# Attention's product with v: f32 exponentials as the moving operand instead of f16 pairs as weights

## The chip, the cores and the metric

The kernel runs on one core of a Trainium2 chip. The metric is the device time of one execution in microseconds; three executions of the kernel before took 1527.67 to 1531.33 us, median 1530.16. The engines are named as in the profile: PE is TensorE (matmuls; PEld its weight loads), DVE is VectorE, ACT is ScalarE, POOL is GpSimd, SP is SyncE, which issues DMAs. TensorE works on weights, which lie in the array, and on a moving operand that streams past them a column at a time; results go to PSUM, which has 8 banks.

## The reference

Attention with cluster masks, then two MoE layers; all inputs are f32.

```python
# attention: batch 2, 8 heads, 768 positions, head_dim 64, 16 centroids per head
q_assign = np.argmax(np.einsum('bhsd,hcd->bhsc', q_n, c_n), axis=-1)   # q_n, k_n, c_n: normalized
k_assign = np.argmax(np.einsum('bhsd,hcd->bhsc', k_n, c_n), axis=-1)
mask = q_assign[:, :, :, None] == k_assign[:, :, None, :]
scores = scale * np.matmul(q, k.transpose(0, 1, 3, 2))
scores = np.where(mask, scores, -1000000000.0)
scores = scores - np.max(scores, axis=-1, keepdims=True)
attn = np.exp(scores)
attn = attn / (np.sum(attn, axis=-1, keepdims=True) + 1e-09)
x = np.matmul(attn, v)                                  # rearranged to 1536 x 512
# first MoE: h = x @ w_in; x = (h * clip(h + 3, 0, 6) / 6) @ w_out
# second MoE: 8 experts relu(x @ w1[e]) @ w2[e], weighted by a balanced softmax of x @ w_gate
```

## The kernel before, in words

f32 precision is kept with pairs of f16 numbers: a value is split into its f16 rounding and the f16 of the rest, and a product of two values takes three f16 matmuls (hi x hi, hi x lo, lo x hi).

Attention runs over 16 heads (`i`), two to a pair (`p`), and over 6 tiles of 128 keys each (`c`); one tile of one head is a unit, numbered `g`, 96 in all. The loop at L952 writes out the instructions of all engines in a fixed order, unit by unit; each engine then works through its own list in that order. In iteration `g` stand:

- `max_unit` for the unit 8 ahead (L659): two matmuls of 384 columns write the masked scores that are needed for the row maximum to the tile `pmt`, two banks of PSUM which exist once, and VectorE reduces them (L675). The next unit's matmuls overwrite `pmt`.
- `e_split` for the unit before (L732): the exponentials E, f32, are cast to f16 (Eh, on ScalarE, every fourth or so on VectorE, L738), and GpSimd subtracts (El, L742).
- `s_mm` (L711): four matmuls of 384 columns make the scores of 128 keys and 768 queries, and ScalarE takes the exponential of all 768 (L729).
- `pv_mm` for the unit 4 behind (L745, the distance is `LAG`): the product with v. Weights are blocks of 128 queries of Eh and El, moving is v: 65 columns (v's high part and a column of ones, which sums the exponentials) and 64 (its low part). The result `pv` lies with queries on partitions. In a head's last unit the term `Wt` is added, which makes good for rows whose cluster has no key.
- `weave` (L695): preparation steps of later pairs at the units that the table `PLACE` names (f16 splits of q and k, cluster choice, v's pair in `vhi` and `vlo`, the sums `abs1` and `abs2` behind `Wt`), the decoding of the first MoE weight (`w00`), and a head's evacuation (`evac_tasks`, L774): division by the sum, f16 split, and transposing DMAs into `xT` (L800).

A step that waits on an engine holds up all that stands behind it on that engine. Behind the loop the first MoE layer's matmuls follow (`l1_mm`, L898; 36 of them don't need the last pair's `xT`).

Of the kernel before, what the change touches and what calls it, by code (L numbers as in the profile page):

```python
# [31 lines left out]
def attention_moe_kernel(  # L32
# [39 lines left out]
    one = const.tile([P, 1], F32, name="one")  # L72

# [327 lines left out]
    ps_s = actx.enter_context(tc.tile_pool(name="ps_s", bufs=2, space=PSUM))  # L401
    ps_v = actx.enter_context(tc.tile_pool(name="ps_v", bufs=2, space=PSUM))
# [3 lines left out]
    NU = NHEAD * NJ  # L406
    qnA = [ap1.tile([P, 2 * NJ, P], F16, name=f"qnA{i}") for i in range(NA)]
    knA = [ap1.tile([P, 2 * NJ, P], F16, name=f"knA{i}") for i in range(2)]
    Wt = [ap1.tile([P, 2, 130], F16, name=f"Wt{i}") for i in range(2)]
# [62 lines left out]
    def prep_tasks(p, parts=None):  # L472
# [47 lines left out]
        def vhi():  # L520
            vn = d["vn"] = ap3.tile([P, 2 * NJ, 130], F16, tag="vn", name=f"vn{p}")
            nc.scalar.activation(vn[:, :, 0:D], vr, AF.Copy, scale=sv[0][:, 0:1])
            nc.gpsimd.memset(vn[:, :, D:D + 1], 1.0)

        def vlo():
            vn = d["vn"]
            nc.vector.scalar_tensor_tensor(
                out=vn[:, :, D + 1:2 * D + 1], in0=vr, scalar=sv[0][:, 0:1], in1=vn[:, :, 0:D],
                op0=ALU.mult, op1=ALU.subtract)
# [129 lines left out]
    def max_unit(i, j):  # L659
# [7 lines left out]
        ps = ps_s.tile([P, 2, 512], F32, tag="s", name=f"pm{i}_{j}") if early else pmt  # L667
# [41 lines left out]
    pvt = {}  # L709

    def s_mm(i, c):  # L711

        p, hh = divmod(i, 2)
        d = st[p]
        ps = ps_s.tile([P, 2, 512], F32, tag="s", name=f"pS{i}_{c}")
# [4 lines left out]
        for g in range(2):  # L720
            nc.tensor.matmul(
                ps[:, g, 0:N2], lhsT=d["kB"][:, t, :], rhs=qb[:, hh * S + g * N2:hh * S + (g + 1) * N2],
                start=True, stop=False)
        for g in range(2):
            nc.tensor.matmul(  # L725
                ps[:, g, 0:N2], lhsT=d["kA"][0:KR, t, :], rhs=qa[0:KR, g * N2:(g + 1) * N2],
                start=False, stop=True)
        E = ap2.tile([P, 2, N2], F32, tag="E", name=f"E{i}_{c}", bufs=3)
        nc.scalar.activation(E, ps[:, :, 0:N2], AF.Exp, scale=d["esc"][:, 0:1])  # L729
        EE[i, c] = E  # L730

    def e_split(i, c):  # L732
        E = EE.pop((i, c))
        Eh = ap3.tile([P, 2, N2], F16, tag="Eh", name=f"Eh{i}_{c}", bufs=5)
        El = ap3.tile([P, 2, N2], F16, tag="El", name=f"El{i}_{c}", bufs=5)
        n = NJ * i + c
        if n % 12 in (0, 3, 5) or n >= NU - LEAD and n % 2:
            nc.vector.tensor_copy(Eh, E)  # L738
        else:
            nc.scalar.copy(Eh, E)  # L740
        for g in range(2):
            nc.gpsimd.tensor_tensor(out=El[:, g], in0=E[:, g], in1=Eh[:, g], op=ALU.subtract)  # L742
        EE[i, c] = (Eh, El)

    def pv_mm(i, c):  # L745
        p, hh = divmod(i, 2)
        d = st[p]
        if c == 0:
            pvt[i] = ps_v.tile([P, NJ, D + 1], F32, tag="v", name=f"pv{i}")
        ps = pvt[i]  # L750
        Eh, El = (x.rearrange("p a b -> p (a b)") for x in EE.pop((i, c)))
        vn = d["vn"][:, hh * NJ + c, :]

        def acc(j, w, r, lo=False, **kw):
            r = r[:, D + 1:2 * D + 1] if lo else r[:, 0:D + 1]
            kw = {"start": False, "stop": False, **kw}
            nc.tensor.matmul(ps[:, j, 0:r.shape[1]], lhsT=w, rhs=r, skip_group_check=True, **kw)

        for j in range(NJ):
            w = Eh[:, P * j:P * j + P]  # L760
            acc(j, w, vn, start=(c == 0 and j == 0))
            acc(j, w, vn, lo=True)
        for j in range(NJ):
            acc(j, El[:, P * j:P * j + P], vn)
        if c == NJ - 1:
            for j in range(NJ):
                w = d[f"qA2_{hh}"][0:D + C, j, :]
                r = Wt[p % 2][0:D + C, hh]
                acc(j, w, r)
                acc(j, w, r, lo=True, stop=(j == NJ - 1))  # L770
# [42 lines left out]
    nc.gpsimd.memset(one, 1.0)  # L813
    c0()
# [103 lines left out]
    LAG = 4  # L918
    tasks, evacs = {}, {}
# [23 lines left out]
    for c in range(FA):  # L943
# [6 lines left out]
        if c + 2 < FA:  # L950
            at(u + 3, wcols[c + 2][1][0])
    for g in range(-LEAD, NU + LAG + 16):  # L952
        i, u = divmod(g, NJ)
        chains = []
        if 0 <= g + LEAD < NU:
            chains.append(max_unit(*divmod(g + LEAD, NJ)))
        if 0 <= g - 1 < NU:
            e_split(*divmod(g - 1, NJ))
        if 0 <= g < NU:
            s_mm(i, u)  # L960
# [7 lines left out]
        if 0 <= gp < NU:  # L968
            pv_mm(*divmod(gp, NJ))
        if 0 <= gp < NU and gp % NJ == NJ - 1:  # L970
            for n, f in enumerate(evac_tasks(gp // NJ)):
                evacs.setdefault(g + (1, 2, 2)[n], []).append(f)
# [670 lines left out]
```

## Time and profile before

| | |
|---|---|
| Median of three runs | 1530.16 us |
| Span of the profiled execution | 1526.7 us |
| Lowest and highest run | 1527.67 and 1531.33 us |
| PE, DVE, ACT, POOL busy over the span | 93%, 63%, 44%, 25% |
| POOL El L742 | 192 instructions, 189.3 us |
| Granted clock in the slices of 38 us up to 305 us | 0.7 to 0.9, from then on nearly always 0.9 or more |

The profiled execution's own time is its span and some 1 us around it (the fastest run is 0.97 us above the span). The shares are averages over a short part in which no engine is full (attention, the first fifth of the span) and a long one in which PE is. A view by windows gives for each stretch the busy time of PE, PEld, DVE, ACT and POOL, the number of instructions in brackets, then the mean granted clock (1 is 2.4 GHz), the DMA's share and GB/s. A timeline row has its start and its length in us, engine, line, operation, out<-in, the shape, how many it stands for, and in brackets the idle time before it. A group's row ends with busy us and mean ns of one, and behind the bar with idle time before it and what ended that. A PE record's length goes on past the point at which the next matmul starts, so the distance of two starts is what a matmul costs.

### The profile page before, as it was taken

The page shows a single profiled execution, that of the slowest core. Times are in us where ns is not written, and L with a number is a line of the kernel's source. Part 1 is how long each engine was busy: PE and PEld are TensorE (multiplying, and loading weights), DVE is VectorE, ACT ScalarE, POOL GpSimd, SP SyncE. Part 2 cuts the span into 40 slices and gives each one's busy share as a digit, 9 for nine tenths or more (in the row PEclk, how much of TensorE's full clock was granted, in tenths as well). Part 3 has the DMA queues.
Part 4 walks back from the last instruction along what each step waited for, and adds up shares of the span by engine and source line. Part 5 has one row for each costly group of instructions (what it writes and reads, how often), then busy time and mean ns, then how long its engine had stood idle before and what let it go on. Part 6 is the DMA issues. An engine that isn't in the chain of part 4 may idle for free.

```text
span 1526.7 us, 22967 instructions
## 1 busy us (share of the span) xinstructions
PE 1418.7 (93%) x9289; PEld 764.8 (50%) x9289; DVE 955.4 (63%) x1732; ACT 665.3 (44%) x1123; POOL 387.8 (25%) x427
## 2 busy tenths in 40 slices
PE   3878888898999998999999999999999999999998
PEld 1555556543444444544555555555555555555554
DVE  7889898876756866466565466466456565564333
ACT  2677777475553444343344333333333333324221
POOL 1579889752101321030030020020020020021000
PEclk9799899898999998999999999999999999999999
DMA  9675743331321100101101101101101101100011
GB/s 217 145 162 102 134 87 62 91 116 52 129 69 56 56 0 1 55 1 56 56 1 55 56 1 56 56 1 56 55 1 55 56 1 55 38 19 1 1 42 42
DMA packets 106633, 87.60 MB, mean 57 GB/s; under 512 B 78368, under 2 KB 88608, under 8 KB 106528
## 3 DMA queue, kind: packets, MB, share of 16 engines
q1 hardware_dynamic: 106528, 86.15, 20.8%
q8 instruction: 72, 1.18, 0.3%
q14 instruction: 33, 0.27, 0.1%
HBM read 64.01 MB, written 3.15 MB: 44 GB/s over the span
## 4 chain that ended last, share of the span: by engine, by line
PE 71%; DVE 17%; ACT 5%; issue 4%; DMA 1%; POOL 0%; DVEq 0%; ACTq 0%; POOLq 0%; SPq 0%
PE o L1471 11%; PE o L1472 11%; PE o L1470 11%; PE X L1521 5%; PE X L1524 5%; PE X L1523 5%; PE Y L1521 4%; PE Y L1524 4%; PE Y L1523 4%; DVE pmt L675 3%; PE l L1248 2%; PE pmt L672 1%; PE l L912 1%; PE l L913 1%; PE l L914 1%
## 5 line engine op out<-in xcount | busy, mean ns | idle before, releaser
L1472 PE MATMUL o<-w_s,hl 128*128 128x512 f16 x768 | 291.6, 380 | 0.0
L1471 PE MATMUL o<-w_s,hh 128*128 128x512 f16 x768 | 291.5, 380 | 0.0
L1470 PE MATMUL o<-w_s,hh 128*128 128x512 f16 x768 | 291.3, 379 | 0.0
L1540 ACT ACTIVATE hh<-u 128x384 f16<-128x384 f32 x192 | 100.3, 522 | 374.9 <-DVE u L1536 374.9
L742 POOL TENSOR_TENSOR El<-E,Eh 128x384 f16<-128x384 f32 x192 | 189.3, 1014 | 72.8 <-DVE Eh L738 41.2
L1541 DVE SCALAR_TENSOR_TENSOR hl<-u,hh 128x384 f16<-128x384 f32 x192 | 112.8, 587 | 120.1 <-ACT hh L1540 120.1
L1536 DVE TENSOR_TENSOR u<-X,snap 128x384 f32<-128x384 f32 x64 | 35.7, 557 | 189.5 <-PE X L1524 189.5
L121 POOL PARTITION_ALL_REDUCE w_m<-w_mx x14 | 5.4, 383 | 570.2 <-DVE w_mx L1336 332.7
L1523 PEld LDWEIGHTS <-wop 128*128 128x128 f16 x896 | 87.9, 98 | 93.6 <-issue 13.5
L1521 PEld LDWEIGHTS <-wop 128*128 128x128 f16 x896 | 87.9, 98 | 81.9 <-issue 1.1
L1536 DVE TENSOR_TENSOR u<-Y,snap 128x384 f32<-128x384 f32 x128 | 70.8, 553 | 80.1 <-PE Y L1524 79.1
L1472 PEld LDWEIGHTS <-hl 128*128 128x128 f16 x768 | 75.2, 98 | 90.8 <-issue 0.3
L1248 PE MATMUL l<-hh,w_s 128*128 128x512 f16 x384 | 118.3, 379 | 0.0
L1524 PEld LDWEIGHTS <-wop 128*128 128x128 f16 x896 | 87.9, 98 | 58.5 <-issue 0.9
L729 ACT ACTIVATE E<-pS,esc 128x768 f32<-128x768 f32 x96 | 86.2, 900 | 65.7 <-PE pS L725 48.4
L1470 PEld LDWEIGHTS <-hh 128*128 128x128 f16 x768 | 76.0, 99 | 66.5 <-issue 0.2
L1529 ACT COPY snap<-X 128x384 f32<-128x384 f32 x128 | 61.2, 478 | 109.7 <-PE X L1524 108.3
L1471 PEld LDWEIGHTS <-hh 128*128 128x128 f16 x768 | 75.2, 98 | 66.5 <-issue 0.2
L675 DVE TENSOR_REDUCE pmt<-pmt 128x1 f32<-128x768 f32 x84 | 80.6, 960 | 19.5 <-PE pmt L672 18.7
L672 PE MATMUL pmt<-kA,qA 80*128 80x384 f16 x184 | 52.1, 369 | 42.5 <-DVE pmt L675 14.2
L1248 PEld LDWEIGHTS <-w_s 128*128 128x128 f16 x576 | 56.4, 98 | 67.5
L1521 PE MATMUL X<-xop,wop 128*128 128x384 f16 x256 | 83.8, 327 | 6.8 <-ACT snap L1529 5.5
(280 smaller groups left out, 2990.5 us busy)
## 6 DMA issues: line engine op xcount, KB each, us to landing
w_raw<-in_moe_w_dram SPq DMA_DIRECT2D x16, 2048.0 KB, 8.2
w_c<-in_moe_w_out_dram SPq DMA_DIRECT2D x16, 512.0 KB, 3.5
w00x<-in_moe_w_in_dram SPq DMA_DIRECT2D x8, 512.0 KB, 5.6
w00f<-in_moe_w_in_dram SPq DMA_DIRECT2D x8, 512.0 KB, 4.1
w_c<-in_moe_w_in_dram SPq DMA_DIRECT2D x8, 512.0 KB, 3.8
qraw<-in_q_dram SPq DMA_DIRECT2D x8, 384.0 KB, 3.8
kraw<-in_k_dram SPq DMA_DIRECT2D x8, 384.0 KB, 4.8
vraw<-in_v_dram SPq DMA_DIRECT2D x2, 1536.0 KB, 10.6
```

The source lines that it names most:

```text
L675: nc.vector.tensor_reduce(nmx[i][:, j:j + 1], ps[:, :, 0:N2], axis=AX.XY, op=ALU.max, negate=True)
L742: nc.gpsimd.tensor_tensor(out=El[:, g], in0=E[:, g], in1=Eh[:, g], op=ALU.subtract)
L1248: nc.tensor.matmul(po[i], lhsT=a, rhs=r, start=(f == 0 and z == 0), stop=(f == NFC - 1 and z == 2))
L1470: nc.tensor.matmul(pe2[t], lhsT=a, rhs=wh, start=first, stop=False)
L1471: nc.tensor.matmul(pe2[t], lhsT=a, rhs=wl, start=False, stop=False)
L1472: nc.tensor.matmul(pe2[t], lhsT=b, rhs=wh, start=False, stop=last)
L1521: nc.tensor.matmul(o[:, 0:XT], lhsT=wh, rhs=xh, start=(first and c == 0), stop=False, skip_group_check=True)
L1523: nc.tensor.matmul(o[:, 0:XT], lhsT=wh, rhs=xl, start=False, stop=False, skip_group_check=True)
L1524: nc.tensor.matmul(o[:, 0:XT], lhsT=wl, rhs=xh, start=False, stop=(c == 1), skip_group_check=True)
L1536: nc.vector.tensor_tensor(h, src, r[k], op=ALU.add)
L1540: nc.scalar.activation(hh, src, AF.Relu)
L1541: nc.vector.scalar_tensor_tensor(out=hl, in0=src, scalar=0.0, in1=hh, op0=ALU.max, op1=ALU.subtract)
```

## The change

The f16 pairs of the exponentials and of v are gone. The work is cut in halves `h` of 384 queries, 192 in all; within a head first the six key tiles of the first half, then those of the second. The scores of a half are two matmuls, its exponential is one of 384 columns. In the product with v the weights are v itself in f32 with two columns of ones (66 columns, `DW`), and the moving operand is E in f32, 384 columns. The result `pvT` has the 64 numbers and the sum on partitions and queries along the columns; `turn_tasks` copies it to SBUF on ScalarE and turns it back with three f32 transposes on PE per half, one and two units after the half's end, and the evacuation starts two units later than before (`TURN`). `Wt` is the weight of two f16 matmuls of 384 columns per half. The sums behind `Wt` are taken from v's sum over all keys, which GpSimd makes (`vsum`). PSUM is dealt anew: three one-bank tiles for scores, three for products. The tuple `SPLIT`, which would leave heads with the old pairs, is empty.

```diff
-    ps_s = actx.enter_context(tc.tile_pool(name="ps_s", bufs=2, space=PSUM))
-    ps_v = actx.enter_context(tc.tile_pool(name="ps_v", bufs=2, space=PSUM))
+    ps_v = actx.enter_context(tc.tile_pool(name="ps_v", bufs=3, space=PSUM))
...
+    DW = D + 2
+    SPLIT = ()
...
+            vn = d["vn"] = ap3.tile([P, 2 * NJ, DW], F32, tag="vn", name=f"vn{p}")
             nc.scalar.activation(vn[:, :, 0:D], vr, AF.Copy, scale=sv[0][:, 0:1])
...
-        def vlo():
+        def vsum():
+            vn = d["vn"].rearrange("p (h j) d -> p h j d", h=2)[:, :, :, 0:D]
+            t = ap2.tile([P, 2, 3, D], F32, tag="vs", name=f"vs{p}", bufs=1)
+            nc.gpsimd.tensor_tensor(out=t, in0=vn[:, :, 0:3], in1=vn[:, :, 3:6], op=ALU.add)
+            nc.gpsimd.tensor_tensor(out=t[:, :, 0], in0=t[:, :, 0], in1=t[:, :, 1], op=ALU.add)
+            nc.gpsimd.tensor_tensor(out=t[:, :, 0], in0=t[:, :, 0], in1=t[:, :, 2], op=ALU.add)
...
+            nc.tensor.matmul(
+                ps[:, :, 0:D], lhsT=one.to_broadcast([P, P]), rhs=t[:, :, 0], start=True, stop=True,
+                skip_group_check=True)
...
+    def s_mm(h):
+        i, x = divmod(h, 2 * NJ)
+        g, c = divmod(x, NJ)
...
+        nc.tensor.matmul(
+            ps, lhsT=d["kB"][:, t, :], rhs=qb[:, hh * S + g * N2:hh * S + (g + 1) * N2], start=True, stop=False)
+        nc.tensor.matmul(
+            ps, lhsT=d["kA"][0:KR, t, :], rhs=qa[0:KR, g * N2:(g + 1) * N2], start=False, stop=True)
+        E = ap2.tile([P, N2], F32, tag="E", name=f"E{h}", bufs=11)
+        nc.scalar.activation(E, ps, AF.Exp, scale=d["esc"][:, 0:1])
...
+        ps = pvT[i, g][0:DW]
+        nc.tensor.matmul(ps, lhsT=d["vn"][:, hh * NJ + c, :], rhs=E, start=(c == 0), stop=False)
         if c == NJ - 1:
+            q = qa.rearrange("p a b -> p (a b)")[0:D + C, g * N2:(g + 1) * N2]
+            nc.tensor.matmul(ps, lhsT=W[:, 0:DW], rhs=q, start=False, stop=False)
+            nc.tensor.matmul(ps, lhsT=W[:, DW:2 * DW], rhs=q, start=False, stop=True)
+
+    def turn_tasks(i, g):
+        x = {}
+        def t0():
+            o = x["o"] = ap2.tile([P, N2], F32, tag="oT", name=f"oT{i}_{g}")
+            nc.scalar.copy(o[0:DW], pvT.pop((i, g))[0:DW])
+        def t1():
+            if g == 0:
+                pvt[i] = ps_v.tile([P, NJ, DW], F32, tag="v", name=f"pv{i}")
+            for n in range(NJ // 2):
+                nc.tensor.matmul(
+                    pvt[i][:, 3 * g + n, :], lhsT=x["o"][0:DW, P * n:P * n + P], rhs=ident[0:DW, 0:DW],
+                    is_transpose=True, start=(g == 0 and n == 0), stop=True, skip_group_check=True)
+        return [t0, t1]
```

How the instructions stand on the engines, at two places. On PE in the loop's middle (unit 50 of the kernel before: the scores' second part and the product with v of unit 46, of whose 18 matmuls the first four stand here; names carry the head and tile, and behind them a number):

```order
L725 LDWEIGHTS kA4_2058
L725 MATMUL pS8_2_2789<-qA2_8_2585,kA4_2058 128x384
L725 LDWEIGHTS kA4_2058
L725 MATMUL pS8_2_2789<-qA2_8_2585,kA4_2058 128x384
L757 LDWEIGHTS Eh7_4_2643
L757 MATMUL pv7_2609<-vn3_1133,Eh7_4_2643 128x65
L757 LDWEIGHTS Eh7_4_2643
L757 MATMUL pv7_2609<-vn3_1133,Eh7_4_2643 128x64
L757 LDWEIGHTS Eh7_4_2643
L757 MATMUL pv7_2609<-vn3_1133,Eh7_4_2643 128x65
L757 LDWEIGHTS Eh7_4_2643
```

In the changed kernel, from the end of unit 50 into unit 51 (E, pS and halves have one number; E93 is the second half of iteration 46, pv7 gets the three transposes of the turn):

```order
L781 MATMUL pvT7_1_1972<-E93_1886,vn3_928 66x384
L798 MATMUL pv7_2022<-ident_69,oT7_0_2001 128x66 x3
L678 LDWEIGHTS qA4_1523
L678 MATMUL pmt_102<-kA4_1525,qA4_1523 128x384
L678 LDWEIGHTS qA4_1523
L678 MATMUL pmt_102<-kA4_1525,qA4_1523 128x384
L728 LDWEIGHTS kB4_1245
L728 MATMUL pS102_2029<-qB4_1204,kB4_1245 128x384
L730 LDWEIGHTS kA4_1525
L730 MATMUL pS102_2029<-qA2_8_1864,kA4_1525 128x384
L781 MATMUL pvT7_1_1972<-E94_1906,vn3_928 66x384
```

The 18 matmuls with their 18 weight loads became one f32 matmul behind each half's scores, and the transposes stand between the units, ahead of the next `pmt`.

On DVE, iterations 54 to 56 of the kernel before: reduces of `pmt` with what stands between them:

```order
L675 TENSOR_REDUCE pmt_101<-pmt_101 128x1
L738 CAST Eh8_5_3013<-E8_5_2934 128x768
L575 TENSOR_REDUCE a_mx6_3043<-sim6_2954 128x24
L675 TENSOR_REDUCE pmt_101<-pmt_101 128x1
L383 SCALAR_TENSOR_TENSOR w0_0_s_132<-w00t0_2724,w00_s_2719,w0_0_s_132 128x4x128
L579 TENSOR_TENSOR a_eq6_3079<-sim6_2954,a_mx6_3043 128x384
L675 TENSOR_REDUCE pmt_101<-pmt_101 128x1
```

The same place after (the three rows of x_r and x_f are head 7's evacuation):

```order
L588 TENSOR_REDUCE a_mx6_2168<-sim6_2093 128x24
L819 TENSOR_SCALAR x_r7_2170<-pv7_2022 128x6
L820 RECIPROCAL x_r7_2170<-x_r7_2170 128x6
L821 TENSOR_TENSOR x_f7_2171<-pv7_2022,x_r7_2170 128x384
L681 TENSOR_REDUCE pmt_102<-pmt_102 128x1
L384 SCALAR_TENSOR_TENSOR w0_0_s_134<-w00t0_1951,w00_s_1946,w0_0_s_134 128x4x128
L592 TENSOR_TENSOR a_eq6_2192<-sim6_2093,a_mx6_2168 128x384
L681 TENSOR_REDUCE pmt_102<-pmt_102 128x1
```

The cast Eh between two reduces is gone, and the evacuation of a head has moved behind the cluster maximum a_mx.

## Rows read from the trace of the kernel before

**Rows 1.** Timeline: the loop's first product with v, what follows it.

```profile
51.61 0.64 PE L757 MATMUL pv<-vn,Eh 128*128 128x65 f16 x12
...
296.91 0.38 PE L912 MATMUL l<-xT,w_s 128*128 128x512 f16 x1
...
298.73 2.61 SPq L800 DMA_TRANSPOSE xT<-xn  x2
```

**Rows 2.** Windows: busy time of each engine, granted clock.

```profile
46.00:57.00 11.00, 9.82 (x97) 6.37 (x95) 8.21 (x23) 9.35 (x13) 5.88 (x7) 1.00 0.19 59
57.00:297.00 240.00, 196.23 (x2793) 141.88 (x2794) 208.31 (x354) 168.57 (x230) 207.28 (x216) 0.88 0.53 106
297.00:335.00 38.00, 38.00 (x180) 17.25 (x177) 29.64 (x52) 24.96 (x45) 14.83 (x11) 1.00 0.41 135
```

**Rows 3.** Waits of PE from 46 to 297: total, times, longest.

```profile
PE pmt L672 <- DVE pmt L675: 14.2, 19, 2.4
PE pmt L672 <- DVE a_oh L590: 7.5, 5, 2.2
...
PE pv L757 <- DVE Wt L633: 3.1, 6, 0.6
PE pmt L672 <- DVE a_eq L582: 3.0, 2, 1.9
PE pS L725 <- DMA qA<-qnA: 2.9, 2, 2.4
```

**Rows 4.** Timeline of PE: one unit of the loop.

```profile
208.24 0.48 PE L672 MATMUL pmt<-kA,qA 80*128 80x384 f16 x2
...
209.22 0.53 PE L757 MATMUL pv<-vn,Eh 128*128 128x65 f16 x12
209.59 0.34 PE L757 MATMUL pv<-vn,El 128*128 128x65 f16 x6
212.32 0.48 PE L672 MATMUL pmt<-kA,qA 80*128 80x384 f16 x1 [2.39 <-DVE pmt L675]
```

**Rows 5.** Timeline of DVE beside it.

```profile
208.11 1.26 DVE L738 CAST Eh<-E 128x768 f16<-128x768 f32 x1
...
211.31 0.95 DVE L675 TENSOR_REDUCE pmt<-pmt 128x1 f32<-128x768 f32 x1
```

**Rows 6.** Groups of PE: small f32 matmuls.

```profile
L91 PE MATMUL X<-b_cs,one 128*128 128x8 f32 x2 | 0.4, 266 | 0.6 <-ACT snap L1529 0.6
L86 PE MATMUL red<-ident,wg_r 128*128 128x1 f32 x2 | 0.4, 260 | 0.4 <-DVE wg_r L81 0.4
```

**Rows 7.** Timeline, PEld and PE: an f32 weight load, its matmuls.

```profile
665.89 0.35 PEld L91 LDWEIGHTS Y<-b_cs,one 128*128 128x128 f32 x2
...
666.05 0.28 PE L91 MATMUL Y<-b_cs,one 128*128 128x8 f32 x2
```

**Rows 8.** Timeline of PE: an f32 transpose.

```profile
641.99 0.27 PE L76 MATMUL Y<-ident,pad 128*128 128x128 f32 x1
642.10 0.38 PE L1470 MATMUL o<-w_s,hh 128*128 128x512 f16 x1
```

**Rows 9.** Groups of DVE from 46 to 297.

```profile
L738 DVE CAST Eh<-E 128x768 f16<-128x768 f32 x26 | 22.5, 865 | 3.4 <-ACT E L729 3.2
L527 DVE SCALAR_TENSOR_TENSOR vn<-vraw,v_s,vn 128x768 f16<-128x768 f32 x8 | 10.0, 1248 | 0.0
```

**Rows 10.** Timeline of DVE: one operation, POOL busy, then idle.

```profile
290.79 1.13 DVE L187 TENSOR_SCALAR w00t<-w00t 128x512 f32<-128x512 f32 x1
...
299.21 0.42 DVE L187 TENSOR_SCALAR w00t<-w00t 128x512 f32<-128x512 f32 x1
```

**Rows 11.** Groups of ACT: first two 46 to 297, last whole span.

```profile
L729 ACT ACTIVATE E<-pS,esc 128x768 f32<-128x768 f32 x94 | 84.4, 900 | 62.0 <-PE pS L725 44.7 <-POOL El L742 10.1 <-DVE ab L628 2.2
L740 ACT CAST Eh<-E 128x768 f16<-128x768 f32 x68 | 56.3, 828 | 1.4
...
L1540 ACT ACTIVATE hh<-u 128x384 f16<-128x384 f32 x192 | 100.3, 522 | 374.9 <-DVE u L1536 374.9
```

More of the change, by code (lines that the diff above doesn't have):

```diff
@@ L72, in attention_moe_kernel @@
     one = const.tile([P, 1], F32, name="one")
+    one16 = const.tile([P, 1], F16, name="one16")
     def red_rows(ps, start=True):
@@ L406, in attention_moe_kernel @@
     NU = NHEAD * NJ
+    DW = D + 2
+    SPLIT = ()
     qnA = [ap1.tile([P, 2 * NJ, P], F16, name=f"qnA{i}") for i in range(NA)]
     knA = [ap1.tile([P, 2 * NJ, P], F16, name=f"knA{i}") for i in range(2)]
-    Wt = [ap1.tile([P, 2, 130], F16, name=f"Wt{i}") for i in range(2)]
+    Wt = [ap1.tile([P, 2, 2 * DW], F16, name=f"Wt{i}") for i in range(2)]
     CT = ap1.tile([P, 3, P], F16, name="CT")
@@ L666, in max_unit @@
         early = NJ * i + j < LEAD and j % 2
-        ps = ps_s.tile([P, 2, 512], F32, tag="s", name=f"pm{i}_{j}") if early else pmt
+        ps = ps_s.tile([P, 2, 512], F32, tag="pm", name=f"pm{i}_{j}") if early else pmt
         t = hh * NJ + j
@@ L719, in s_mm @@
         qa = d[f"qA2_{hh}"].rearrange("p a b -> p (a b)")
[L720 to L743, printed above, removed]
@@ L745, in pv_mm, with e_split @@
-    def pv_mm(i, c):
+        nc.tensor.matmul(
[4 more added lines that the diff above has]
+        nc.scalar.activation(E, ps, AF.Exp, scale=d["esc"][:, 0:1])
+        EE[h] = E
+    def e_split(h):
+        E = EE[h]
+        if h // (2 * NJ) not in SPLIT:
+            return
+        Eh = ap3.tile([P, N2], F16, tag="Eh", name=f"Eh{h}", bufs=8)
+        El = ap3.tile([P, N2], F16, tag="El", name=f"El{h}", bufs=8)
+        nc.scalar.copy(Eh, E)
+        nc.gpsimd.tensor_tensor(out=El, in0=E, in1=Eh, op=ALU.subtract)
+        EE[h] = (Eh, El)
@@ L746, in pv_mm @@
+    def pv_mm(h):
+        i, x = divmod(h, 2 * NJ)
+        g, c = divmod(x, NJ)
         p, hh = divmod(i, 2)
         d = st[p]
-        if c == 0:
[L749 to L764, printed above, removed]
-        if c == NJ - 1:
[L766 to L770, printed above, removed]
+        E = EE.pop(h)
@@ new lines, in pv_mm, with acc @@
+        qa = d[f"qA2_{hh}"]
+        W = Wt[p % 2][0:D + C, hh]
+        if i in SPLIT:
+            if x == 0:
+                pvt[i] = ps_v.tile([P, NJ, DW], F32, tag="v", name=f"pv{i}")
+            ps = pvt[i]
+            Eh, El = E
+            vn = d["v16", hh][:, c, :]
+            vs = vn[:, 0:D + 1], vn[:, D + 1:2 * D + 1]
+            def acc(j, w, r, **kw):
+                kw = {"start": False, "stop": False, **kw}
+                nc.tensor.matmul(ps[:, j, 0:r.shape[1]], lhsT=w, rhs=r, skip_group_check=True, **kw)
+            for n in range(NJ // 2):
+                w = Eh[:, P * n:P * n + P]
+                acc(3 * g + n, w, vs[0], start=(x == 0 and n == 0))
+                acc(3 * g + n, w, vs[1])
+            for n in range(NJ // 2):
+                acc(3 * g + n, El[:, P * n:P * n + P], vs[0])
+            if x == 2 * NJ - 1:
+                for j in range(NJ):
+                    w = qa[0:D + C, j, :]
+                    acc(j, w, W[:, 0:D + 1])
+                    acc(j, w, W[:, DW:DW + D], stop=(j == NJ - 1))
+            return
@@ L967, in attention_moe_kernel @@
             l1_mm(0, *HEAD[gp - NU + 2], range(KD - 1))
[L968 to L972, printed above, removed]
+        for z in range(2):
+            if 0 <= g < NU:
+                s_mm(2 * g + z)
+            if 0 <= 2 * g + z - 1 < 2 * NU:
+                e_split(2 * g + z - 1)
+            h = 2 * gp + z
+            if 0 <= gp < NU:
+                pv_mm(h)
+                i, x = divmod(h, 2 * NJ)
+                if x % NJ == NJ - 1:
+                    if i not in SPLIT:
+                        for n, f in enumerate(turn_tasks(i, x // NJ)):
+                            late(f, g + 1 + n)
+                    if x == 2 * NJ - 1:
+                        o = 0 if i in SPLIT else TURN
+                        for n, m in enumerate((1, 2, 2)):
+                            late(lambda i=i, n=n: evac_step(i, n), g + o + m)
         weave(chains, tasks.pop(g, []) + evacs.pop(g, []))
```

76 lines of the change are left out of this document (42 added, 34 removed).

## The prediction

> **What bounds the kernel now.** The attention loop runs from the first product with v at 51.61 us to the first-layer matmul at 296.91 that follows the last [rows 1]: 245.3 us for 96 units (16 heads by 6 tiles of 128 keys). Everything behind it is the two MoE layers, which the change doesn't touch. In the windows from 46 to 297 [rows 2] no engine is full: of the 240 us from 57 on DVE is busy for 208.3, POOL for 207.3, PE for 196.2 and ACT for 168.6, and the mean granted clock is 0.88. TensorE has two levels, 1.2 and 2.4 GHz, so 0.88 means 24% of the stretch, 58 us, at the lower one.
>
> What ends PE's idle time is in the list of waits [rows 3]: above all the masked scores' tile pmt, which is in PSUM once. The first matmuls of a unit overwrite it and wait until VectorE has reduced it, and VectorE works in order. One unit shows it [rows 4, 5]: pmt's two matmuls at 208.24, the four of the scores behind them, the product with v at 209.22 and 209.59, and then nothing until 212.32. VectorE meanwhile had the cast Eh (1.26 us) and two weight steps ahead of the reduce at 211.31. At the upper clock six matmuls of 384 columns take 0.98 us here (208.24 to 209.22), 0.163 each, the 12 with Eh 0.37 and so the 6 with El 0.18. PE needs 0.98 + 0.55 = 1.53 us for a unit, and the loop gives it 245.3 / 96 = 2.56. VectorE feeds PE too slowly; PE is far from its own limit.
>
> **The product with v, the main term.** Before: 18 matmuls of 64 or 65 columns, 0.55 us per unit, 52.8 us in all. After: two f32 products with 384 moving columns per unit, 192 in all. No f32 matmul of that width is in the trace; the price per column comes from small ones [rows 6]. An f32 product is two matmul records. Each lasts 260 ns with 1 column and 266 with 8: 0.86 ns per column. An f16 matmul takes 0.163 us for 384, 0.42 ns per column. So each record streams at half the f16 rate, and a product, being two, costs four times the f16 time: 4 x 0.163 = 0.65 us. 192 x 0.65 = 124.8 us, an addition of 72.0 us. The lower bound is half rate for the whole product, 0.32 us (61 us); the upper adds weight loads that nothing hides. Two f32 loads of 128 columns take 0.35 us, 665.89 to 666.24 [rows 7], so one of the 66 columns here is at most 0.09, and with 384 records that is 35 us. I take 0.65 without it: the product starts at 666.05, inside those 0.35 us, and a load of 0.09 fits under a record of 0.32.
>
> The Trainium skill ("Perfetto Trace Analysis", section Engine Utilization) gives PE's output rate a division by 2 for FP32_LOW_HIGH. Read as the rate of the whole product, that would make the term 61 us and the sum 63.8 us smaller, the second rival's case. Read as the rate of one of the two records it is what the 0.86 ns show. No run here shows which at 384 columns; I follow the records.
>
> **The smaller terms on PE.** The keys' rest term Wt: 12 matmuls in 0.37 us per head become 4 of 384 columns, 0.65: 16 x 0.28 = +4.5 us. The transposed result is turned back by 6 f32 transposes per head; one with 128 columns holds PE for 0.11 us, 641.99 to 642.10 [rows 8]; with 66 columns 0.06 if columns set it, 0.11 if the 128-column load does; at 0.085, 96 of them are +8.2 us (5.8 to 10.6). The sums for fully masked rows (abs) lose 96 matmuls of 129 columns (0.05 each by column) for as many of one column and one f32 product of 128 columns per pair (0.22): -5 to +2, I take 0. Together PE gets 72.0 + 4.5 + 8.2 = 84.7 us more work at the upper clock.
>
> **What PE gets back.** Its present losses are the 43.8 us of idle time in the 240 us [rows 2]; the clock, where 58 us at half rate with PE busy for 82 to 100% cost 24 to 29, say 26; and the starts of the stalls, since a record's end is modelled some 0.17 us after the next could start, which hides 8 us in some 48 waits: 78 us. VectorE loses 26 casts, 22.5 us, and the low part of v, 10.0 [rows 9]. Its SBUF operations also ran long beside the busy POOL: a weight step took 1.13 us at 290.79 and 0.42 at 299.21, with POOL idle [rows 10]. POOL loses its 192 subtractions and gains only v's sums, eight times about 2 us. So VectorE's 216.5 us [rows 2] fall to 184 by the first two alone, some 165 with the third (an estimate: 20 us from the steps that halve). That is 1.7 us per unit against PE's 1.53 + 84.7 / 96 = 2.41, with a unit of slack between pmt's matmuls and the next ones. So the waits on pmt, a_oh and a_eq go nearly whole; waits on the transposing DMA (2.9) and on Wt (3.1) stay, Wt being wanted three units earlier. ScalarE gets 192 exponentials for 96 of 0.90 us; at the 0.52 of a relu of that shape they are 100 us for 86, 32 copies of the same size are 16 more, and 56.3 us of casts go [rows 11]: cheaper. The three one-bank score tiles let it be late by two halves, over 2 us, which a preparation step of 0.93 doesn't use up.
>
> Of the 43.8 idle us I take back 36: the five largest rows on VectorE other than Wt's, from the reduce's 14.2 down to a_eq's 3.0, are 33.0 together, and some 3 belong to El and small ones. Of the clock's 26 I take back 23, which leaves one spell of some 7 us at the lower level, and the 8 behind the stalls: 67 in all, 11 of the 78 stay. The bounds are 30 (most stalls only change their place) and 78.
>
> Late next is PE itself. At the loop's end the turn puts a copy (0.5), three transposes (0.3) and their hops, some 1.6 us, ahead of the evacuation. Now the last transposing DMA ends at 301.34, 4.4 us after the loop [rows 1]; 36 first-layer matmuls of 0.216 us stand behind the loop and last 7.8, so 6.0 is covered. Uncovered are only the transposes' wait for the copy, 0.5 us; without the cover it would be 1.6. Ahead of the first product, ScalarE no longer casts Eh for units 0 to 3 while PE waits: -2 us, between 0 and -3.
>
> **Sum.** 84.7 - 67 + 0.5 - 2 = +16 us. This is a difference to the profiled execution, whose span is 1526.7 us; the median of the runs shown, 1530.16, is 3.4 above that, so the forecast is 1530.16 + 16 = 1546 us. Its own range is 1533 to 1559 (recovery 11 either way, transposes 2).
>
> **Rivals.**
> 1. PE runs without a gap and all 78 us come back: 84.7 - 78 + 0.5 - 2 = +5 with the middle prices, -1 with transposes and abs at their lower ends; I put it at 1532. For: VectorE's 1.7 us per unit is far below PE's 2.41. Against: no stretch of the loop now is without waits, and the DMA's and Wt's stay. 16%.
> 2. The f32 product costs half: 0.32 us. PE's work then grows by only 21 us, to about 1.75 us per unit, VectorE's 1.7 is level with it, and with two thirds of today's losses gone (52 of 78) the loop takes 31 + 2 us less: 1497 us. It decides where 192 products save the forecast's 16 us, below 0.57 us each; above that the change loses. For: no wide f32 matmul is in the trace. Against: 0.86 ns per column in both records. 10%.
> 3. Weight loads aren't hidden: 35 us more at most, some of it in place of waits: +20 to +25, 1568. For: with 8 columns nothing can cover the second load, so no row shows one covered. Against: the first was, by a matmul half as long as a record here. 12%.
> 4. The lower clock stays as often as now. With PE always busy 58 us at half rate cost 29: the 23 counted back are lost and 3 more, 1572. For: it was low for 24% of a stretch in which PE was busy for 82%. Against: from 297 to 335, with PE filled, it is 1.00 [rows 2]. 6%.
>
> **How the numbers follow.** The forecast has 56%. A measurement of this kernel can tell 0.2%, 3 us, from no change. Slower by over that: 54 of the forecast's 56, rivals 3 and 4, and 3 of rival 1: 75%. Within it: 11 of rival 1 and 2 of the forecast: 13%. Faster: rival 2 and 2 of rival 1: 12%. The range for 8 times in 10 reaches down through rival 1 to 1528 and up to rival 3, 1568; left out are rival 2, most of 4 and the upper half of 3.
>
> **What the profile after would show.** Right: the products with v come in pairs of records about 0.32 us apart, 384 of them; PE busy for over 93% of the loop, granted clock 0.97 or more, the loop 255 to 268 us long; pmt's wait on the reduce under 4 us in all; VectorE near 165 us; POOL nearly empty; everything behind the loop shifted as a block, with the same lengths. Wrong: records 0.16 us apart (rival 2), gaps of 0.05 us or more between the records (3), 0.88 again as clock (4), or a new wait of over 5 us, most likely on ScalarE for a score bank, or on Wt.

## The result, and the profile after

The changed kernel takes 1543.8 us (median of 4 runs, 1538.0 to 1545.3) beside 1530.7 for the kernel before in the same session (4 runs, 1527.7 to 1534.5): ratio 1.0072, 95% interval 1.0046 to 1.0099. Run a second time it was 1541.8 (6 runs) at ratio 1.0071 [1.0055, 1.0086]. It is slower by 11 to 13 us; the forecast was 1546, +16. All times below leave out two disturbed executions, 2774 us in run 6 (the one that was profiled, so run 6 has times but no trace to read) and 3095 us in run 8.

The windows of the loop after, in the columns of [rows 2]; the last row is the loop itself:

```profile
46.00:57.00 11.00, 10.62 (x54) 6.01 (x54) 8.16 (x21) 8.61 (x15) 5.24 (x10) 1.00 0.13 33
57.00:297.00 240.00, 234.59 (x1444) 127.04 (x1443) 158.40 (x303) 149.09 (x282) 33.89 (x49) 1.00 0.52 105
297.00:335.00 38.00, 35.33 (x157) 15.72 (x156) 22.97 (x40) 18.51 (x33) 8.92 (x8) 0.96 0.34 108
...
50.52:303.25 252.73, 247.32 (x1510) 133.46 (x1508) 164.91 (x315) 155.50 (x292) 38.16 (x57) 1.00 0.50 102
```

PE is busy for 234.6 of the 240 us where it was 196.2, and the granted clock is 1.00 where it was 0.88. Work on POOL falls from 207 us to 34. The bound has changed its engine: before, PE waited for VectorE; now VectorE waits for PE, 55.3 us ahead of the reduce of pmt where it was 18.7, as the group of DVE's costliest line in the loop says, first before, then after (busy, mean, idle before and its releaser):

```profile
L675 DVE TENSOR_REDUCE pmt<-pmt 128x1 f32<-128x768 f32 x84 | 80.6, 960 | 19.5 <-PE pmt L672 18.7
L681 DVE TENSOR_REDUCE pmt<-pmt 128x1 f32<-128x768 f32 x84 | 81.0, 965 | 56.2 <-PE pmt L678 55.3
```

One unit on PE, the counterpart of [rows 4]:

```profile
200.74 0.49 PE L678 MATMUL pmt<-kA,qA 80*128 80x384 f16 x2
201.07 0.33 PE L728 MATMUL pS<-qB,kB 128*128 128x384 f16 x1
201.23 0.33 PE L730 MATMUL pS<-qA,kA 82*128 82x384 f16 x1
201.40 0.81 PE L781 MATMUL pvT<-E,vn 128*66 128x384 f32 x2
202.04 0.33 PE L728 MATMUL pS<-qB,kB 128*128 128x384 f16 x1
202.21 0.33 PE L730 MATMUL pS<-qA,kA 82*128 82x384 f16 x1
202.37 0.81 PE L781 MATMUL pvT<-E,vn 128*66 128x384 f32 x2
203.02 0.49 PE L678 MATMUL pmt<-kA,qA 80*128 80x384 f16 x2
...
205.30 0.35 PE L798 MATMUL pv<-ident,oT 66*128 66x66 f32 x3
205.48 0.33 PE L678 MATMUL pmt<-kA,qA 80*128 80x384 f16 x1
```

Read the starts, since a busy time includes the modelled end of the last matmul. The product's two records start at 201.40 and what follows them at 202.04: 0.64 us beside 0.16 for an f16 matmul of the same 384 columns, so 0.32 for a record. pmt comes again after 2.28 us with no gap, where [rows 4] has 2.39 us of waiting in one unit. Three transposes take 0.18. PEld has the product's two weight loads done at 201.54, while the records run:

```profile
201.24 0.30 PEld L781 LDWEIGHTS pvT<-E,vn 128*66 128x66 f32 x2
```

PE's waits from 46 to 310, where [rows 3] had 14.2 us for the reduce, which is no longer in the list, and 7.5 for a_oh:

```profile
PE red L87 <- DVE qk_r L82: 2.3, 6, 0.4
PE l L945 <- DVE x_f L821: 2.0, 1, 2.0
PE pmt L678 <- DVE a_oh L603: 1.4, 1, 1.4
...
PE pmt L678 <- DVE a_eq L595: 0.7, 1, 0.7
```

The second one is new and lies behind the loop. PE at the loop's end, and what DVE does there:

```profile
303.08 0.32 PE L785 MATMUL pvT<-qA,Wt 80*66 80x384 f16 x1
304.03 0.40 PE L798 MATMUL pv<-ident,oT 66*128 66x66 f32 x3 [0.62 <-ACT oT L792]
306.48 0.39 PE L945 MATMUL l<-xT,w_s 128*128 128x512 f16 x1 [2.05 <-DVE x_f L821]
306.71 0.40 PE L946 MATMUL l<-xT,w_s 128*128 128x512 f16 x1
306.92 0.61 PE L947 MATMUL l<-xT,w_s 128*128 128x512 f16 x1
307.32 0.63 PE L945 MATMUL l<-xT,w_s 128*128 128x512 f16 x1
```

```profile
304.58 0.43 DVE L188 TENSOR_SCALAR w00t<-w00t 128x512 f32<-128x512 f32 x1 [5.15 <-ACT w00t L183]
305.04 0.43 DVE L189 TENSOR_SCALAR w00t<-w00t 128x512 uint32<-128x512 uint32 x1
305.38 0.16 DVE L819 TENSOR_SCALAR x_r<-pv 128x6 f32<-128x6 f32 x1
305.57 0.19 DVE L820 RECIPROCAL x_r<-x_r 128x6 f32<-128x6 f32 x1
305.87 0.56 DVE L821 TENSOR_TENSOR x_f<-pv,x_r 128x384 f32<-128x384 f32 x1
```

The first-layer matmul that should fill the turn (L945) itself waits 2.05 us for x_f, the step that releases the last head's PSUM bank, and two weight steps stand ahead of that step in VectorE's queue. From 306.9 on the starts are 0.43 us apart instead of 0.22: in this execution the granted clock was at the lower level to 310.3.

The difference by place, after less before: first product with v -1.1 us (50.52 for the 51.61 of [rows 1]); end of the loop +6.3, so the loop itself is 7.4 longer (252.7 for 245.3); a matmul of the first layer's fill behind the turn +11.3 (312.1 for 300.8); after PE's next long wait, for the scale of a weight (w_r), +9.8 (358.1 for 348.3); span +9.3. The medians differ by 1.4 to 4 us more: the executions differ in how long the MoE layers run at the lower clock (13.6 us of it behind the fill in this profile, 20.4 before, 27.2 in the second profile of after, whose span is 1541.6).

### The profile page after: what moved, and what is told of

Its sections match the earlier page's. It is cut to its first block, busy times and chain, and to the rows that moved or that the text cites. A ratio compares the mean times of both kernels' runs of the same rounds, so it can differ in the third digit from the quotient of the medians.

```text
span 1536.0 us, 20136 instructions
## 1 busy us (share of the span) xinstructions
PE 1466.4 (95%) x7929; PEld 752.8 (49%) x7929; DVE 905.3 (59%) x1681; ACT 647.1 (42%) x1182; POOL 210.9 (14%) x260
## 3 DMA queue, kind: packets, MB, share of 16 engines
q1 hardware_dynamic: 106528, 86.15, 20.4%
## 4 chain that ended last, share of the span: by engine, by line
PE 82%; DVE 10%; ACT 4%; DMA 2%; issue 2%; SPq 0%; POOL 0%; DVEq 0%; ACTq 0%; POOLq 0%
PE o L1525 11%; PE o L1524 11%; PE o L1526 11%; PE pvT L781 8%; PE X L1575 5%; PE X L1578 5%; PE X L1577 5%; PE Y L1575 4%; PE Y L1578 4%; PE Y L1577 4%; PE l L1302 2%; PE pmt L678 2%; PE pS L730 2%; PE pS L728 2%; PE l L945 1%
## 5 line engine op out<-in xcount | busy, mean ns | idle before, releaser
L781 PE MATMUL pvT<-E,vn 128*66 128x384 f32 x384 | 154.9, 486 | 0.0
L733 ACT ACTIVATE E<-pS,esc 128x384 f32<-128x384 f32 x192 | 110.5, 580 | 93.5 <-PE pS L730 92.3
L681 DVE TENSOR_REDUCE pmt<-pmt 128x1 f32<-128x768 f32 x84 | 81.0, 965 | 56.2 <-PE pmt L678 55.3
L1575 PE MATMUL X<-xop,wop 128*128 128x384 f16 x256 | 83.8, 327 | 6.5 <-ACT snap L1583 5.2
L1575 PE MATMUL X<-xT,wop 128*128 128x384 f16 x256 | 83.4, 326 | 1.3 <-DVE lg_r L82 1.3
L1578 PE MATMUL X<-xop,wop 128*128 128x384 f16 x256 | 83.8, 328 | 0.0
```

The costliest lines, as they stand in the source:

```text
L733: nc.scalar.activation(E, ps, AF.Exp, scale=d["esc"][:, 0:1])
L781: nc.tensor.matmul(ps, lhsT=d["vn"][:, hh * NJ + c, :], rhs=E, start=(c == 0), stop=False)
L1575: nc.tensor.matmul(o[:, 0:XT], lhsT=wh, rhs=xh, start=(first and c == 0), stop=False, skip_group_check=True)
L1578: nc.tensor.matmul(o[:, 0:XT], lhsT=wl, rhs=xh, start=False, stop=(c == 1), skip_group_check=True)
```

## Experiments

All ratios are to the kernel before on the same chip in the same session. "After" is 1.0071.

**1. The first layer's accumulators in other banks.**

```diff
-    for n, g in (("ps_b", (2, 3, 6, 7)), ("ps_c", (4, 5))):
+    for n, g in (("ps_c", (3, 4, 5)), ("ps_b", (2, 6, 7))):
```

> The kernel after, with the first layer's first three accumulators laid in banks 3 to 5, which are free since the start of the last rows, instead of banks 2, 3 and 6: 27 of the 36 matmuls that precede the last rows' turn back no longer wait for the bank of the last head's product. In the trace after, TensorE waits there 2.05 us for VectorE's x_f and falls to the lower clock for 3.4 us behind it, some 2 us more. Theory (the step of the tail in the prediction failed because its cover itself waited): the wait goes, the clock stays high over the end of the loop, and the time falls by 3 to 5 us, to about 1540. Rival (the wait only moves to the fourth accumulator or to the last rows of x, since VectorE's turn of the last head is late whatever stands before it): under 1 us, 1543 to 1544.

1536.3 us (11 runs), ratio 1.0042 [1.0029, 1.0055], 0.29% or 4.4 us below after. The fill now starts right behind the transposes:

```profile
303.96 0.32 PE L785 MATMUL pvT<-qA,Wt 80*66 80x384 f16 x1
304.90 0.40 PE L798 MATMUL pv<-ident,oT 66*128 66x66 f32 x3 [0.62 <-ACT oT L792]
305.14 0.38 PE L945 MATMUL l<-xT,w_s 128*128 128x512 f16 x1
```

From the end of the loop to that same matmul of the fill it takes 4.9 us here, 3.9 before, 8.8 in the first profile of after and 7.1 in the second, which has the same 2.05 us wait and no low clock behind it. So the bank's wait is 2 us, the low clock 1.7 more in the executions that have it, and the turn alone 1.0. The theory held.

**2. The product as two f16 matmuls of the same width.**

```diff
...
-        E = ap2.tile([P, N2], F32, tag="E", name=f"E{h}", bufs=11)
+        E = ap2.tile([P, N2], F16, tag="E", name=f"E{h}", bufs=11)
...
-        nc.tensor.matmul(ps, lhsT=d["vn"][:, hh * NJ + c, :], rhs=E, start=(c == 0), stop=False)
+        v16 = d["v16", hh][:, c]
+        nc.tensor.matmul(ps, lhsT=v16[:, 0:DW], rhs=E, start=(c == 0), stop=False)
+        nc.tensor.matmul(ps, lhsT=v16[:, DW:2 * DW], rhs=E, start=False, stop=False)
```

> The kernel after, with each product with v of 128 keys by 384 rows as two f16 matmuls (the high and the low part of v against exponentials that ScalarE writes as f16; the low part of the exponentials is left out) instead of one f32 matmul. Same columns, same order, same accumulators; v's two parts cost ScalarE and GpSimd one more step per head. By the theory that an f32 product is two records at half the f16 rate (0.645 us for 384 columns, where the f16 matmuls of 384 columns beside it take 0.325 by the mean, 0.16 without their wait) the pair of f16 takes 0.32 to 0.33, TensorE gets 192 x 0.32 = 61 us less to do, and the loop falls from 253 us towards 195 to 215, where ScalarE (about 160) and VectorE (165) begin to show: 1490 to 1510 us. Rival (an f32 product was never dearer than its two records at the f16 rate, and the loop is held by something else): the loop changes by less than 15 us, 1530 or above.

1512.4 us, ratio 0.9878 [0.9852, 0.9904]. PE in a unit, then the loop's window:

```profile
201.40 0.33 PE L782 MATMUL pvT<-E,v 128*66 128x384 f16 x1
201.57 0.32 PE L783 MATMUL pvT<-E,v 128*66 128x384 f16 x1
201.73 0.32 PE L728 MATMUL pS<-qB,kB 128*128 128x384 f16 x1
```

```profile
50.95:275.80 224.85, 197.91 (x1509) 124.39 (x1509) 166.20 (x312) 159.16 (x306) 51.41 (x71) 0.99 0.55 114
```

A pair takes 0.33 us for the 0.645 of the f32 product, so 61 us went from PE's work as expected. The loop lost only 28: PE is idle for 27 us again. The time is just above the theory's 1490 to 1510. The price is shown, and so is that waits for VectorE return as soon as PE's unit is short; the largest are these:

```profile
PE red L87 <- DVE qk_r L82: 4.5, 6, 1.8
PE pmt L678 <- DVE pmt L681: 4.5, 8, 1.2
```

VectorE isn't full there: it is busy for 166 of the 225 us and itself waits 39.9 us for pmt from PE. It is late at some units and early at others, so a share of busy time doesn't show that it paces PE.

**3. The f32 product beside the old load of the other engines.**

```diff
-        if h // (2 * NJ) not in SPLIT:
-            return
...
+        n = h // 2
+        if n % 12 in (0, 3, 5) or n >= NU - LEAD and n % 2:
+            nc.vector.tensor_copy(Eh, E)
+        else:
+            nc.scalar.copy(Eh, E)
         nc.gpsimd.tensor_tensor(out=El, in0=E, in1=Eh, op=ALU.subtract)
-        EE[h] = (Eh, El)
```

> The kernel after, with what the change took off the other engines put back beside its f32 product: every exponential is cast to f16 again (26 of 94 units on VectorE, the others on ScalarE) and GpSimd subtracts again, and nothing reads the results. So this is TensorE's part of the change alone; VectorE gets back 22 us of casts and the slower operations beside GpSimd, GpSimd its 186 us. Theory A (the gaps of the loop closed because TensorE's work per unit grew to 2.6 us, past what any other engine needs per unit, whatever these save): the loop stays 253 to 258 us, 1542 to 1549 in all. Theory B (the gaps closed because VectorE and GpSimd were relieved): TensorE idles again 20 us or more before pmt, the loop takes 272 us or more, 1563 and above. The prediction's recovery of 67 of 78 us rested on both; a result between says how much on each.

1563.5 us, ratio 1.0217 [1.0195, 1.0240], 22 us above after. The loop's window:

```profile
51.42:327.90 276.48, 255.35 (x1510) 133.99 (x1508) 212.02 (x370) 206.79 (x427) 216.09 (x245) 0.99 0.45 93
```

Theory B by its number. 21 us of idle time return on PE, at a clock of 0.99, spread over waits for VectorE, the largest being these:

```profile
PE pmt L678 <- DVE qnA L696: 5.7, 5, 1.9
PE red L87 <- DVE qk_r L82: 3.2, 6, 1.3
PE pmt L678 <- DVE a_oh L603: 2.8, 5, 1.6
```

VectorE and GpSimd are loaded as before, 212.0 us (212.5) and 216.1 (212.7), and ScalarE more, 206.8 (173.9); on VectorE v's low part isn't put back, but the casts take 32.2 us for 22.5. TensorE's part of the change alone thus lengthens the loop by 31 us (276.5 for 245.3), and what the other engines save brings 24 of them back.

**5, 6, 9 and 12. Whose load it is.** Each puts back one share, with results that nothing reads: VectorE's 26 units of casts; GpSimd's subtraction (of a zero tile); ScalarE's 70 units of casts; and all casts on ScalarE with the subtraction behind them.

```diff
...
+        if n % 12 in (0, 3, 5) or n >= NU - LEAD and n % 2:
+            Eh = ap3.tile([P, N2], F16, tag="Eh", name=f"Eh{h}", bufs=3)
+            nc.vector.tensor_copy(Eh, E)
```

> The kernel after with only VectorE's share of the old load: 26 of 96 units are cast to f16 on VectorE (0.5 us for each half unit, some 26 us in the loop), nothing reads them; no casts on ScalarE, no subtraction. With all of the old load put back the loop went from 252.6 to 276.3 us at full clock, with TensorE waiting for VectorE's qnA, a_oh, qk_r and pmt. Theory A (VectorE's queue is what delays those steps, so that its own added work is what counts): 10 to 24 us of the 23.7 come from this, 1553 to 1563. Theory B (the casts are hidden, and it is GpSimd's subtraction, which holds the exponentials' buffers and slows VectorE's operations beside it, that opens the gaps): under 5 us, 1543 to 1548.

```diff
...
+        nc.gpsimd.tensor_tensor(out=El, in0=E, in1=zero, op=ALU.subtract)
```

> The kernel after with only GpSimd's share of the old load: each half unit of exponentials has a zero tile subtracted on GpSimd (0.97 us each, 186 us in the loop), nothing reads the result; no casts. By theory A (VectorE's own added work opens the gaps) under 8 us, 1543 to 1551. By theory B (GpSimd's work beside VectorE slows VectorE's first-layer decode and transposed scans, L188 0.42 us after against 0.86 before, and holds the exponentials' buffers longer) 15 to 24 us, 1558 to 1567, with L188 back above 0.8 us and TensorE waiting for VectorE again.

```diff
...
+        if not (n % 12 in (0, 3, 5) or n >= NU - LEAD and n % 2):
+            Eh = ap3.tile([P, N2], F16, tag="Eh", name=f"Eh{h}", bufs=3)
+            nc.scalar.copy(Eh, E)
```

> The kernel after with only ScalarE's share of the old load: 70 of 96 units are cast to f16 on ScalarE (138 half units of 0.50 us, 69 us in the loop), nothing reads them; no casts on VectorE, no subtraction. All of the old load together cost 23.7 us of loop, VectorE's casts alone 4.3 and 2 to 5 in all, GpSimd's subtractions alone some 6 in all. Theory A (the shares add up, so that ScalarE's casts are the missing 12 to 14 us): 1553 to 1560. Theory B (each queue alone has room beside an f32 product of 2.6 us a unit; it is exponential, cast and subtraction in a row, with their buffers, that makes the rest): under 6 us, 1543 to 1550.

```diff
-        if h // (2 * NJ) not in SPLIT:
-            return
...
         nc.scalar.copy(Eh, E)
         nc.gpsimd.tensor_tensor(out=El, in0=E, in1=Eh, op=ALU.subtract)
-        EE[h] = (Eh, El)
```

> The kernel after with ScalarE's and GpSimd's old load in a row, nothing of it on VectorE: every half unit of exponentials is cast on ScalarE (192 of 0.50 us) and GpSimd subtracts the cast from it, nothing reads the result. The three shares alone cost some 2 to 4 us (VectorE's casts), 2 to 4 (ScalarE's) and 6 (GpSimd's), 10 to 14 together; with all three in one kernel it was 20 to 22. Theory A (the rest comes of VectorE's casts, which wait in VectorE's queue for an exponential or a buffer ahead of the steps that TensorE needs; VectorE stood 4.6 us in five waits for GpSimd and 7.1 us in seven for ScalarE there): without them 1546 to 1553. Theory B (the rest comes of exponential, cast and subtraction in a row and the buffers they hold): 1557 or more.

| put back | time, us | ratio | above after |
|---|---|---|---|
| VectorE's casts | 1546.0 | 1.0103 [1.0083, 1.0123] | 0.32%, 5 us |
| GpSimd's subtraction | 1549.0 | 1.0124 [1.0102, 1.0145] | 0.53%, 8 us |
| ScalarE's casts | 1545.8 | 1.0096 [1.0078, 1.0115] | 0.25%, 4 us |
| casts on ScalarE, subtraction | 1555.0 | 1.0154 [1.0133, 1.0176] | 0.83%, 13 us |
| all of it (run 3) | 1563.5 | 1.0217 [1.0195, 1.0240] | 1.46%, 22 us |

Run 5 came out as its theory B, run 6 as its A, run 9 as its B: each says that its own share is not the whole, and run 12 fell between its two theories. Against after's ratio the single shares make 17 us of the 22, and 4 + 8 = 12 of run 12's 13 (which casts all 96 units on ScalarE, not 70). With some 3 us of uncertainty on each, the 5 left over are not shown to be more than noise: no culprit among the three, the shares about add up. One thing does grow when the shares meet: a cast of half a unit on VectorE took 0.39 us in run 5 and 0.62 in run 3, beside GpSimd, 12 us more over 52 casts; whether the 5 us come from that was not tested. What run 12 does show is GpSimd beside VectorE:

```profile
51.95:319.80 267.85, 252.69 (x1510) 133.88 (x1508) 180.85 (x312) 225.59 (x479) 213.87 (x245) 0.99 0.48 97
```

VectorE runs the same instructions as in after, in 180.9 us for 164.9. In run 9, with ScalarE's casts and GpSimd as idle as in after (38.8 us), they took 167.6, so some 13 of the 16 us go with GpSimd's work. The Trainium skill ("Trainium Architecture — The Big Picture", section What this means for kernel authors) says that these two engines share a pair of ports under an exclusive lock; the 13 us agree with that, but no row here shows the lock itself.

**7 and 10. The kernel before with less feeding.** Run 7 leaves out the low part of the exponentials, its subtraction and its six matmuls per unit; run 10 moves VectorE's casts to ScalarE and computes all that before does.

```diff
-        for g in range(2):
-            nc.gpsimd.tensor_tensor(out=El[:, g], in0=E[:, g], in1=Eh[:, g], op=ALU.subtract)
...
-        for j in range(NJ):
-            acc(j, El[:, P * j:P * j + P], vn)
```

```diff
-        if n % 12 in (0, 3, 5) or n >= NU - LEAD and n % 2:
+        if False:
```

> The kernel before without the low part of the exponentials: no subtraction on GpSimd and none of the six matmuls a unit that use it; the casts stay. TensorE gets 576 x 0.0275 = 16 us less to do (a third of 52.8 us less than that in the rows, since they overlap their loads), VectorE the same number of instructions but no GpSimd beside it. Theory (the loop before is held by its feeding, above all by VectorE slowed beside GpSimd): the loop falls by more than TensorE's 16 us, by 30 to 50, to 1480 to 1500. Rival (the feeding is VectorE's own work, which stays, and the loop before is held by that): it falls by 16 us or less, 1512 to 1528.

> The kernel before with all casts of exponentials to f16 on ScalarE: VectorE loses 26 units of 0.865 us, 22.5 us in the loop, ScalarE gets 26 x 0.83 = 21.6 us. Theory (VectorE's own work paces the loop of before, with 216 of 245 us busy): the loop falls by 6 to 15 us, 1516 to 1525. Rival (ScalarE, 203 of 289 us busy over the loop and the start of the first layer, becomes as late as VectorE was): within 4 us of before, 1527 to 1535.

Run 7: 1504.5 us, ratio 0.9833 [0.9814, 0.9851]. Run 10: 1519.5 us, ratio 0.9929 [0.9916, 0.9943], which is 11 us below before and 22 below after, the fastest kernel here that leaves nothing out. Their loops, 7 and then 10:

```profile
50.66:267.40 216.74, 178.30 (x2297) 123.56 (x2295) 183.57 (x360) 171.57 (x237) 27.53 (x32) 0.90 0.60 118
```

```profile
50.68:288.30 237.62, 197.05 (x2872) 143.75 (x2871) 193.94 (x335) 191.63 (x263) 206.75 (x222) 0.89 0.56 108
```

Run 7's loop is 28.6 us shorter, of which 16 are PE's own, so GpSimd's relief returned only 13, and the whole is just short of the theory's 30 to 50. VectorE gained far more than the loop: 183.6 us for 212.5 with the same instructions. The clock stays at 0.90, and PE still waits 13.5 us for the reduce. Run 10 has the reduce's wait down from 14.2 to 5.5 us and a loop shorter by 7.7, with no change to PE's work:

```profile
PE pmt L672 <- DVE a_oh L590: 8.2, 6, 2.5
PE pmt L672 <- DVE qnA L690: 5.7, 4, 1.9
PE pmt L672 <- DVE pmt L675: 5.5, 8, 1.3
```

VectorE's own casts were one pace-maker; the waits on a_oh and qnA, 7.5 and 4.1 before, did not shrink with them.

**4 and 8. Some heads on f16 pairs.** Every second head, then four of sixteen, made of pairs again, with the banks of run 1.

```diff
-    SPLIT = ()
+    SPLIT = tuple(range(1, 16, 2))
...
+        if i in SPLIT:
+            E = ap2.tile([P, N2], F32, tag="Es", name=f"E{h}", bufs=2)
...
```

> Every other head goes back to f16 pairs of exponentials (odd heads, cast on ScalarE, subtracted on GpSimd), the even heads keep the f32 product; the first layer's banks are as in the run with banks 3 to 5. By the rows a head of f32 costs TensorE 12 x 0.645 + 6 x 0.06 + 0.28 = 8.4 us more or less against 3.3 for f16, so TensorE gets 8 x 5.1 = 41 us less to do, ScalarE gets 8 x 5 = 40 us more (155 to 195 of its time in the loop) and GpSimd 8 x 12. Theory (the loop after is bound by TensorE, and one of before by its feeding; in between both fit): the loop falls to 215 to 230 us and the time to 1500 to 1520, below both kernels. Rival (the feeding binds as soon as pairs are made, or the fewer buffers of exponentials, 9 for 11, stall ScalarE): the loop stays above 243 us, 1530 or more.

Run 4: 1584.5 us, ratio 1.0346 [1.0327, 1.0366]: the rival's side, and over 60 us beside the theory. What failed is in ACT's waits:

```profile
ACT E L736 <- POOL Eh L746: 74.3, 74, 2.7
```

With two buffers the next exponential needs the subtraction of the last but one, which needs that one's cast, issued behind an exponential. Run 8 has four for its heads, and eight that the others share with the pairs:

```diff
-    SPLIT = ()
+    SPLIT = (3, 7, 11, 15)
...
+            E = ap2.tile([P, N2], F32, tag="Es", name=f"E{h}", bufs=4)
...
```

> Four of the sixteen heads (3, 7, 11, 15) on f16 pairs with four f32 buffers of exponentials for them instead of two, 8 buffers for the others, and the first layer in banks 3 to 5. In the run with eight such heads ScalarE waited 74.3 us for GpSimd, 74 times, since two buffers let a half unit pass only every exponential, cast and subtraction in a row (0.58 + 0.45 + 0.97 us against 0.9 that TensorE needs for half a unit). Theory (that was buffers, not the division of work): with four, the chain overlaps, TensorE saves 4 x 5.1 = 20 us, GpSimd's 0.97 us for a half unit gives back up to 4: 1516 to 1524, below before. Rival (the pairs stall wherever they are made, since ScalarE is in order behind them): 1536 or more.

It took 1533.3 us, ratio 1.0021 [1.0009, 1.0033], loop 246.7. The stall on GpSimd is gone, as its theory said, but its time is 9 us above the theory's: with 20 us less work on PE the loop is only 6 to 8 shorter than after's; 16 us of idle time are back (230.8 busy of 246.7). ScalarE now stands 56.5 us for buffers that PE has yet to read, but PE's scores wait for an exponential only 0.2 us in all. PE's largest waits are for VectorE:

```profile
PE pmt L678 <- DVE pmt L681: 4.2, 4, 1.8
PE pmt L678 <- DVE a_oh L603: 4.1, 4, 1.4
```

That is read from the waits alone; no run here relieved VectorE beside these pairs.

## Why the prediction was right, and where not

The direction, the mechanism and nearly the size were right, the size partly by luck. Three terms were off: PE's added work and its recovery made the forecast too long, the tail made it too short.

- **The bound before.** Right: moving 22 us of casts from VectorE to ScalarE, and nothing else, shortened the loop by 7.7 us (run 10). That is one of several waits, not the whole of the 44 us.
- **The f32 product at 0.65 us.** Right: 0.645, and the loads are hidden (done at 201.54, and the next matmul starts at 202.04, right behind two records of 0.32). Rivals 2 and 3 are out; run 2 gives the f16 price of the same columns beside it, 0.33 for two. The Trainium skill ("FP8 and Floating Point Precision", section TensorE Precision Notes) counts four passes for true f32, which is the ratio here: 0.645 to 0.163. Rival 2's 1497 was also too low for its own case: run 2 has that price and took 1512, since half of the old losses stayed (a loop of 225 us for 247 - 61 = 186 of work) and not a third.
- **PE's other terms.** Three transposes in 0.18 us, so 0.06 each, the lower bound; 0.085 was 2.4 us too much for 96. In the loop PE is busy for 247.3 us, and by the prediction's count before had 245.3 - 78 = 167.3 of work: 80 us were added, not 84.7. The rest of that difference, 2.3, was not pinned down (abs was counted at nothing, with -5 to +2 around it).
- **What PE gets back.** Under-sized: 78 less the 5.4 us still idle is some 73, not 67. The clock was 1.00 from 51 to 303 us, so all of its 26 came back and not 23, and the waits on a_oh and a_eq shrank to 2.1. That is rival 1's mechanism, in the loop: predicted +17.7 there, measured +7.4 (+9.3 in the second profile, 254.6, whose first two products still take 1.28 us each). The reason was half named. Run 3 shows 49 of the 73 from PE's longer unit alone (80 - 31), and 24 from the relief of the others. About half of the 49 is the clock, at 0.99 there, the rest idle time, 21 us for 45, so the longer unit hides waits. VectorE's 165 us came out at 164.9, and run 7 bears out the part of GpSimd in it: 29 us less on VectorE, of which the casts are 6 and v's low part 2, so 21 in the other steps for the estimated 20.
- **The tail.** This step failed: "36 first-layer matmuls of 0.216 us stand behind the loop and last 7.8, so 6.0 is covered". The cover was there by its length, but PE is in order, and the first of those matmuls wrote a bank that only the end of the covered chain releases. Uncovered were 3.2 to 4.9 us and not 0.5; run 1 gives 1.0 once the banks are others.
- **The start.** -2 predicted, -1.1 measured.
- **The sum.** -1.1 + 7.4 + 4.9 = +11.2 at the fill, of which some 1.5 were regained by the wait for the weight's scale. The forecast's +16 was as near as it was by luck: a loop too long by 10 us met a tail too short by 3 to 4.
- **Signs in the profile.** Pairs 0.32 apart, PE over 93% (97.9), clock 1.00, pmt's wait on the reduce gone, POOL nearly empty: all seen. The loop, 252.7, lies just below the 255 to 268 given, and what stands behind it didn't shift quite as a block (+11.3, +9.8, +9.3). Rival 4 is out by the clock. The exponentials took 0.58 us each, not 0.52; ScalarE had 97 us to spare, so this cost nothing.

## What to carry to other kernels

Moving work onto the engine that waits takes back its waiting first: here 80 us of new work cost 7 in the loop. But price that recovery by both causes, the longer unit that hides waits and the relief of the engines that fed it, and expect the waits back when the unit is made shorter again (runs 2 and 8). When work is to cover a wait, check what its first instruction needs, its PSUM bank too, and not only how long it lasts. And before a stage is rebuilt, try to move the load of the pacing engine: one condition changed in run 10 was worth more than anything that the rebuilt product gave.

## What the runs showed of the hardware

- An f32 product of 384 columns is two records of 0.32 us, each half the f16 rate, so four f16 matmuls' time; its weight loads of 66 columns are hidden (201.24 to 201.54 in the unit shown).
- Three f32 transposes of 66 columns took 0.18 us, 0.06 each, where one of 128 columns took 0.11 before [rows 8]: the price goes with the columns, not with the weight load of 128 columns that both have.
- VectorE's same instructions in the loop of before took 212.5 us beside a GpSimd busy for 212.7, and 183.6 with it busy for 27.5 (run 7).
- The same 2.05 us wait of PE was followed by 3.4 us at the lower clock in one execution and by none in another, so a low spell behind one wait can't be counted on in either direction.
